# Interleaving the two MLP layers by half batch, with PSUM tiles drawn from one single-bank and one double-bank pool

## The chip, the cores and the metric

The kernel runs on one core of a Trainium2 chip. Its engines appear in the profile as PE (TensorE, matrix products and transposes), DVE (VectorE), ACT (ScalarE), POOL (GpSimd) and SP (SyncE, which here only issues DMAs). PE writes its results to PSUM; ACT and DVE read them from there and write to SBUF. The metric is the device time in microseconds (us), the median of three runs.

## The reference, cut to what matters

Inputs are `q`, `k` and `v` of shape 4 x 8 x 768 x 64 (batch, heads, positions, head width), all float32. Attention keeps, for each query, the 6 chunks of 32 keys with the highest upper bound; then a layer norm and a two-layer MLP follow, with a residual:

```python
k_min, k_max = min and max of k over each chunk of 32 keys
ub = sum(maximum(q * k_min, q * k_max), axis=-1)        # masked to causal chunks
top_chunks = argsort(ub)[..., -6:]
scores = (q @ k.T) / sqrt(64), kept where the key's chunk is selected and key <= query
attn_out = softmax(scores) @ v
x = attn_out as (4, 768, 512)
xn = (x - mean) / sqrt(var + 1e-6) * g_ln
out = x + maximum(xn @ w_ch1, 0) @ w_ch2                # 512 -> 2048 -> 512
```

## The kernel before

**Units of work.** Attention is cut into 16 groups `g`: batch `b = g // 4` and a pair of heads. A group's 768 positions are six tiles of 128, in two halves `r = 0, 1` of three tiles each. A group goes through `load_qk` and `load_v` (DMA), `prep_q` and `prep_k` (PE transposes into PSUM tiles `tr`, evacuated by ACT and DVE into the rings QA, QB, KA, KB), `bounds` (PE, tile `ub`), `select` (DVE), `mask_t` (PE transposes into `trh`, copied by DVE into QA and QB), and for each half `scores` (PE into tile `mm`, then an exponential on ACT into `pt`), `diag` (POOL zeroes the upper triangle of `pt`), `values` (PE into tile `sm`) and `normalise` (DVE divides and writes the group's columns of `x_all`).

**The MLP of a batch** follows when its four groups are done: `stats` (DVE: mean, variance and the centred `xc`), `x_t` (PE transposes of `xc` into `trh`, scaled into `xT` by DVE or ACT), `rstd` (DVE and POOL), `mlp1` (16 calls; each makes two 128-row slices of the hidden layer for one half, 8 matmuls into a tile `mm`, then a ReLU on ACT into `hT`), `mlp2` (24 calls; four calls of 4 matmuls make the 128 output rows of one position tile `s`, and after the fourth DVE adds the residual into `ot`, which SP stores to memory).

**PSUM.** There are three pools of two buffers. `ps_t` holds `tr` and both kinds of `trh`; `ps_s` holds `ub` and `sm`; `ps_m` holds tiles of `[P, 2, 512]` float32, a double bank each, shared by `scores`, `mlp1` and `mlp2`. A tile of `mlp2` (`yps[b]`, line 464) takes a whole double bank for two position tiles, so it stays open for eight calls:

```python
        if j == 0 and s % 2 == 0:
            yps[b] = ps_m.tile([P, 2, 512], F32, name="mm", tag="mm")
        yp = yps[b][:, s % 2]
```

**Order.** Every call is registered with a due time by `at(t, ...)`; the calls are issued in the order of these times, and a scheduler beneath them then settles the order of the instructions on each engine and hands a pool's free buffers to its tiles. An engine executes its instructions in that order. One unit of due time is one group. Group `g` starts its scores at `T = g - 4`, plus `GAP = 1.5` from the second batch on. The MLP of batch `b` is spread from the end of the attention of batch `b` to the end of that of `b + 1`: all 16 calls of `mlp1` in the first half of that time, all 24 of `mlp2` in the second. So the first batch's attention has no MLP beside it, the attention of batches 1 to 3 runs beside the MLP of the batch before, and the MLP of the last batch stands alone at the end (the tail). `x_all`, `xc`, `xT` and `hT` are tiles of a whole batch; `x_all` is float16.

Of the kernel before, what the change touches and what calls it, by code (L numbers as in the profile page):

```python
# [10 lines left out]
ALU = mybir.AluOpType  # L11
# [8 lines left out]
def kernel(  # L20
# [39 lines left out]
    ring = ctx.enter_context(tc.tile_pool(name="ring", bufs=1))  # L60
    ldp = ctx.enter_context(tc.tile_pool(name="ldp", bufs=4))
    vap = ctx.enter_context(tc.tile_pool(name="vap", bufs=5))
    prp = ctx.enter_context(tc.tile_pool(name="prp", bufs=2))
    smp = ctx.enter_context(tc.tile_pool(name="smp", bufs=2))
    ptp = ctx.enter_context(tc.tile_pool(name="ptp", bufs=2))
    xp = ctx.enter_context(tc.tile_pool(name="xp", bufs=2))
    xcp = ctx.enter_context(tc.tile_pool(name="xcp", bufs=1))
    htp = ctx.enter_context(tc.tile_pool(name="htp", bufs=1))
    outp = ctx.enter_context(tc.tile_pool(name="outp", bufs=2))

    PSUM = bass.MemoryType.PSUM
    ps_t = ctx.enter_context(tc.tile_pool(name="ps_t", bufs=2, space=PSUM))
    ps_s = ctx.enter_context(tc.tile_pool(name="ps_s", bufs=2, space=PSUM))
    ps_m = ctx.enter_context(tc.tile_pool(name="ps_m", bufs=2, space=PSUM))
# [13 lines left out]
    hsel = const.tile([P, 2], F32, name="hsel", tag="hsel")  # L88
    mhalf = const.tile([P, NT], F32, name="mhalf", tag="mhalf")
    NK = 5  # L90
    QA = [ring.tile([P, S], F16, name=f"QA{i}", tag=f"QA{i}") for i in range(NK)]
# [74 lines left out]

    def xb(b):
        if b not in x_tiles:
            x_tiles[b] = (
                xp.tile([P, NT, H, D], F16, name="x_all", tag="x_all"),  # L170
                xp.tile([P, KT1, S], F16, name="xT", tag="xT"),
            )
        return x_tiles[b]

# [23 lines left out]
    def turn(g, nm, t0, t1):  # L198
        pst = ps_t.tile([P, 512], F32, name="tr", tag="tr")
        src = st[g][nm]  # L200
        for t in range(t0, t1):
            nc.tensor.transpose(pst[:, (t - t0) * P:(t - t0 + 1) * P], src[:, t, :, :], ident_f)  # L202
        return pst[:, 0:(t1 - t0) * P]
# [65 lines left out]
    def bounds(g):  # L269
        p, bd = st[g], BD[g % NB]  # L270
        if g < HP:
            ub = ps_s.tile([P, NT - 1, 2, NCH], F32, name="ub", tag="sm")
            nc.tensor.matmul(
                ub.rearrange("p s h c -> p (s h c)"), ident_b, causb.rearrange("p s h c -> p (s h c)"),
                start=True, stop=False,
            )
            for s in range(1, NT):
                o = ub[:, s - 1].rearrange("p h c -> p (h c)")
                for nm, arr in (("q32", 0), ("r32", 1)):
                    nc.tensor.matmul(  # L280
                        o, p[nm][:, s * P:(s + 1) * P], bd[:, arr].rearrange("p h c -> p (h c)"),
                        start=False, stop=(s == NT - 1 and arr == 1),
                    )
        else:
            bh = BH[g % NB]
            ub = ps_s.tile([P, NT - 1, 2, 2, NCH], F32, name="ub2", tag="sm")
            for s in range(1, NT):
                o = ub[:, s - 1].rearrange("p l h c -> p (l h c)")
                for i, (nm, arr) in enumerate((("qh", 0), ("ql", 0), ("rh", 1), ("rl", 1))):
                    nc.tensor.matmul(  # L290
                        o, p[nm][:, s * P:(s + 1) * P], bh[:, arr].rearrange("p l h c -> p (l h c)"),
                        start=(i == 0), stop=(i == 3),
                    )
# [19 lines left out]
    def mask_t(g, i):  # L313
        mn = MN[i % NM]
        pm = ps_t.tile([P, S], F16, name="trh", tag="tr")
        for s in range(NT - 1):
# [60 lines left out]
    def values(g, r):  # L377
        pt, va = st[g]["pt", r], st[g]["va"]
        pv = ps_s.tile([P, 2, TR, D + 1], F32, name="sm", tag="sm")
        st[g]["pv", r] = pv  # L380
# [9 lines left out]
    def normalise(g, r):  # L390
        b, hp = divmod(g, HP)
        x_all, _ = xb(b)
        pv = st[g]["pv", r]
        rden = smp.tile([P, 2, TR, 1], F32, name="rden", tag="rden")
        nc.vector.reciprocal(rden, pv[:, :, :, D:D + 1])  # L395
        nc.vector.tensor_tensor(  # L396
            x_all[:, TR * r:TR * r + TR, 2 * hp:2 * hp + 2, :].rearrange("p s h d -> p h s d"),
            pv[:, :, :, 0:D], rden.to_broadcast([P, 2, TR, D]), ALU.mult,
# [3 lines left out]

    rs = {}

    def stats(b, t0, t1):
        x_all, _ = xb(b)
        if t0 == 0:
            rs[b] = dict(
                st=smp.tile([P, NT, nc.vector.BN_STATS_DIM], F32, name="bst", tag="bst"),
                mv=smp.tile([P, NT, 2], F32, name="mv", tag="mv"),  # L410
                rstd=smp.tile([P, NT], F32, name="rstd", tag="rstd"),
                xc=xcp.tile([P, NT, DM], F16, name="xc", tag="xc"),
            )
        r = rs[b]
        for s in range(t0, t1):
            xs = x_all[:, s].rearrange("p h d -> p (h d)")
            nc.vector.bn_stats(r["st"][:, s], xs)
            nc.vector.bn_aggr(r["mv"][:, s, :], r["st"][:, s])
            nc.vector.tensor_scalar(r["xc"][:, s, :], xs, r["mv"][:, s, 0:1], None, op0=ALU.subtract)

    def rstd(b, t0, t1):

        r = rs[b]
        c = slice(t0, t1)
        ve = smp.tile([P, NT], F32, name="ve", tag="ve")
        nc.vector.tensor_scalar(
            ve[:, c], r["mv"][:, c, 1], HS * HS, HS * HS * LN_EPS, op0=ALU.mult, op1=ALU.add,
        )
        nc.gpsimd.tensor_tensor(r["rstd"][:, c], ve[:, c], mhalf[:, c], ALU.pow)

    def x_t(b, kt, r):
        _, xT = xb(b)
        px = ps_t.tile([P, TR * P], F16, name="trh", tag="tr")
        for i in range(TR):
            nc.tensor.transpose(  # L435
                px[:, i * P:(i + 1) * P], rs[b]["xc"][:, TR * r + i, kt * P:(kt + 1) * P], ident_h,
            )
        c = slice(TR * r * P, TR * (r + 1) * P)
        if b == 0 and kt % 2 == 0:
            nc.scalar.activation(xT[:, kt, c], px, ACTF.Copy, scale=gstr[:, kt:kt + 1])  # L440
        else:
            nc.vector.tensor_scalar(xT[:, kt, c], px, gstr[:, kt:kt + 1], None, op0=ALU.mult)

    hts = {}

    def mlp1(b, r, m):
        _, xT = xb(b)
        if b not in hts:
            hts[b] = htp.tile([P, KT2, S], F16, name="hT", tag="hT")
        c = slice(TR * r * P, TR * (r + 1) * P)  # L450
        hp_ = ps_m.tile([P, 2, 512], F32, name="mm", tag="mm")
        for i in range(2):
            for kt in range(KT1):
                nc.tensor.matmul(  # L454
                    hp_[:, i, 0:TR * P], w1b[:, kt, (m + i) * P:(m + i + 1) * P],
                    xT[:, kt, c], start=(kt == 0), stop=(kt == KT1 - 1),
                )
        nc.scalar.activation(hts[b][:, m:m + 2, c], hp_[:, :, 0:TR * P], ACTF.Relu, scale=HS)  # L458

    yps = {}  # L460

    def mlp2(b, s, j):
        if j == 0 and s % 2 == 0:
            yps[b] = ps_m.tile([P, 2, 512], F32, name="mm", tag="mm")
        yp = yps[b][:, s % 2]
        for kt in range(4 * j, 4 * j + 4):
            nc.tensor.matmul(  # L467
                yp, hts[b][:, kt, s * P:(s + 1) * P], w2b[:, kt, :],
                start=(kt == 0), stop=(kt == KT2 - 1),
            )  # L470
        if j == 3:
            x_all, _ = xb(b)
            ot = outp.tile([P, DM], F32, name="ot", tag="ot")
            nc.vector.scalar_tensor_tensor(  # L474
                ot, yp, rs[b]["rstd"][:, s:s + 1], x_all[:, s].rearrange("p h d -> p (h d)"),
                op0=ALU.mult, op1=ALU.add,
            )
            nc.sync.dma_start(out[b, s * P:(s + 1) * P, :], ot)


    at(-9.0, consts_first)
    at(-8.95, g_load)
    GAP = 1.5
    for g in range(NG):
# [24 lines left out]
    for i in range(2, NK):  # L509
        at(-4.3 + 0.3 * i, ring_init, i)  # L510
    for b in range(B):
        e = 4.0 * b + (GAP if b > 0 else 0.0)
        for r in range(NR):
            f = e + (-0.56 if r == 0 else 0.0)
            for s in range(TR * r, TR * (r + 1)):
                at(f, stats, b, s, s + 1)
            for kt in range(KT1):
                at(f + 0.01, x_t, b, kt, r)
        at(e + 0.2, rstd, b, 0, NT)
        e = e + 0.05  # L520
        d = 4.0 * (b + 1) + GAP + 0.05 - e
        if b == B - 1:
            d = 4.0
        for m in range(KT2):
            at(e + 0.05 + 0.5 * d * m / KT2, mlp1, b, m // 8, 2 * m % KT2)
        for n in range(24):
            at(e + 0.06 + 0.5 * d + 0.5 * d * n / 24, mlp2, b, n // 4, n % 4)

# [32 lines left out]
```

## Time and profile before

| | us |
|---|---|
| runs | 330.22, 330.78, 332.76; median 330.78 |
| the profiled execution | 332.52 |
| its span, first to last instruction | 330.8 |
| PE, DVE, ACT, POOL busy in the span | 301.0, 203.9, 180.1, 74.0 |

The profiled execution is 1.7 us above the median and has 1.7 us around its span. Matrix products are pipelined: a product's own duration in the profile (326 ns for the first layer's) is longer than the time to the next one's start, so busy PE time says little, and the pace has to be read from starts. The largest groups by line, with the mean duration of one:

| line | what | count | mean ns |
|---|---|---|---|
| L454 | PE, first layer, 128x384 | 512 | 326 |
| L467 | PE, second layer, 128x512 | 384 | 379 |
| L359 | PE, scores | 448 | 251 |
| L385 | PE, values | 672 | 195 |
| L365 | ACT, exponential of scores | 96 | 916 |
| L458 | ACT, ReLU of the first layer | 64 | 810 |
| L474 | DVE, residual | 24 | 745 |
| L417, L418, L419 | DVE, stats | 24 each | 676, 164, 344 |
| L396 | DVE, normalise | 32 | 555 |

The DMAs move 26.65 MB, most of it in the first 75 us.

### The profile page before, as it was taken

The page shows a single profiled execution, that of the slowest core. Times are in us where ns is not written, and L with a number is a line of the kernel's source. Part 1 is how long each engine was busy: PE and PEld are TensorE (multiplying, and loading weights), DVE is VectorE, ACT ScalarE, POOL GpSimd, SP SyncE. Part 2 cuts the span into 40 slices and gives each one's busy share as a digit, 9 for nine tenths or more (in the row PEclk, how much of TensorE's full clock was granted, in tenths as well). Part 3 has the DMA queues.
Part 4 walks back from the last instruction along what each step waited for, and adds up shares of the span by engine and source line. Part 5 has one row for each costly group of instructions (what it writes and reads, how often), then busy time and mean ns, then how long its engine had stood idle before and what let it go on. Part 6 is the DMA issues. An engine that isn't in the chain of part 4 may idle for free.

```text
span 330.8 us, 6794 instructions
## 1 busy us (share of the span) xinstructions
PE 301.0 (91%) x2708; PEld 199.2 (60%) x2708; DVE 203.9 (62%) x657; ACT 180.1 (54%) x261; POOL 74.0 (22%) x116
## 2 busy tenths in 40 slices
PE   3879887999999998999999999999999999899994
PEld 2668675666675664666766565666656455565441
DVE  7766755998857779896564759886634336700121
ACT  2436759677975475358685625377775332366000
POOL 9714835211131422230313131120101020100000
PEclk9999989999999999999999999999999999999999
DMA  9997999963435636424523050000000101000021
GB/s 163 190 187 139 194 195 214 190 146 68 95 26 127 96 93 104 92 45 95 74 51 24 34 87 34 34 33 2 2 0 2 63 34 63 35 0 2 32 95 63
DMA packets 81967, 26.65 MB, mean 81 GB/s; under 512 B 76304, under 2 KB 78352, under 8 KB 81936
## 3 DMA queue, kind: packets, MB, share of 16 engines
q1 hardware_dynamic: 53632, 18.88, 24.1%
q0 software_dynamic: 27776, 7.34, 22.2%
q8 instruction: 21, 0.34, 0.5%
q10 hardware_dynamic: 528, 0.00, 0.1%
q14 instruction: 10, 0.08, 0.1%
HBM read 27.27 MB, written 6.29 MB: 101 GB/s over the span
## 4 chain that ended last, share of the span: by engine, by line
PE 60%; ACT 19%; DVE 15%; issue 2%; DMA 1%; SPq 0%; POOL 0%; ACTq 0%
PE mm L454 20%; PE mm L467 18%; ACT pt L365 8%; PE mm L359 6%; ACT hT L458 5%; PE sm L385 4%; PE ub L280 4%; PE tr L202 3%; ACT KB L254 3%; ACT KA L253 2%; DVE ot L474 2%; PE ub L290 2%; DVE kc L251 2%; DVE kc L252 2%; PE trh L435 2%
## 5 line engine op out<-in xcount | busy, mean ns | idle before, releaser
L365 ACT ACTIVATE pt<-mm 128x1024 f16<-128x1024 f32 x96 | 86.8, 916 | 52.1 <-PE mm L359 51.5
L454 PE MATMUL mm<-xT,w1b 128*128 128x384 f16 x512 | 93.3, 326 | 4.7 <-ACT hT L458 3.2
L467 PE MATMUL mm<-w2b,hT 128*128 128x512 f16 x384 | 92.7, 379 | 2.5 <-DVE ot L474 1.7
L458 ACT ACTIVATE hT<-mm 128x768 f16<-128x768 f32 x64 | 51.8, 810 | 40.7 <-PE mm L454 40.2
L454 PEld LDWEIGHTS <-w1b 128*128 128x128 f16 x512 | 49.0, 98 | 32.3 <-issue 5.5
L467 PEld LDWEIGHTS <-hT 128*128 128x128 f16 x384 | 36.6, 98 | 37.0 <-issue 3.7
L372 POOL TENSOR_SCALAR_AFFINE_SELECT pt<-pt 128x768 f16<-128x768 f16 x32 | 28.2, 880 | 115.4 <-ACT pt L365 115.4
L474 DVE SCALAR_TENSOR_TENSOR ot<-mm,rstd,x_all 128x512 f32<-128x512 f32 x24 | 17.9, 745 | 44.6 <-PE mm L467 43.1
L359 PE MATMUL mm<-QA,KA 128*128 128x128 f16 (+2 forms) x224 | 35.9, 251 | 5.2 <-ACT pt L365 4.3
L359 PE MATMUL mm<-QB,KB 128*128 128x128 f16 (+2 forms) x224 | 35.4, 252 | 0.0
L385 PE MATMUL sm<-va,pt 128*128 128x65 f16 x672 | 33.0, 195 | 2.3 <-ACT pt L365 1.8
L385 PEld LDWEIGHTS <-pt 128*128 128x128 f16 x672 | 28.4, 99 | 9.4 <-ACT pt L365 3.5
L193 POOL DMA_DIRECT2D va<-in_v_dram x32 | 28.2, 883 | 1.1 <-issue 0.2
L395 DVE RECIPROCAL rden<-sm 128x6 f32<-128x6 f32 x32 | 6.2, 193 | 33.5 <-PE sm L385 33.4
L253 ACT CAST KA<-tr 64x512 f16<-64x512 f32 (+1 forms) x32 | 15.0, 468 | 17.3 <-DVE kc L252 17.2
L359 PEld LDWEIGHTS <-KA 128*128 128x128 f16 x224 | 19.0, 102 | 8.9 <-issue 2.3
L202 PE MATMUL tr<-ident_f,qn 128*128 128x128 f32 x96 | 18.7, 303 | 5.9 <-DMA qn<-in_q_dram 5.1
L359 PEld LDWEIGHTS <-KB 128*128 128x128 f16 x224 | 18.6, 101 | 6.7 <-issue 4.2
L202 PE MATMUL tr<-ident_f,kn 128*128 128x128 f32 x96 | 19.7, 306 | 1.6 <-DMA kn<-in_k_dram 0.7
L251 DVE TENSOR_REDUCE kc<-tr 128x16 f32<-128x512 f32 (+1 forms) x32 | 17.7, 552 | 3.1 <-PE tr L202 2.9
L396 DVE TENSOR_TENSOR x_all<-sm,rden 128x384 f16<-128x384 f32 x32 | 17.7, 555 | 0.8
L226 DVE SCALAR_TENSOR_TENSOR q<-tr,q 128x384 f16<-128x384 f32 (+1 forms) x24 | 11.7, 488 | 9.9 <-ACT q L225 9.6
(79 smaller groups left out, 339.8 us busy)
## 6 DMA issues: line engine op xcount, KB each, us to landing
qn<-in_q_dram SPq DMA_DIRECT2D x32, 192.0 KB, 3.7
kn<-in_k_dram SPq DMA_DIRECT2D x32, 192.0 KB, 3.8
out_dram<-ot SPq DMA_DIRECT2D x24, 256.0 KB, 2.0
va<-in_v_dram POOLq DMA_DIRECT2D x32, 96.0 KB, 5.2
w1b<-in_moe_w_ch_dram POOLq DMA_DIRECT2D x4, 512.0 KB, 7.8
w2b<-in_moe_w_ch_dram POOLq DMA_DIRECT2D x4, 512.0 KB, 8.2
gstr<-in_moe_g_ln_dram ACTq DMA_DIRECT2D x1, 2.0 KB, 3.4
```

Of the source, the lines that this page charges most:

```text
L193: nc.gpsimd.dma_start(va[:, hh, t0:t1, 0:D], v[b, 2 * hp + hh, t0 * P:t1 * P, :].rearrange("(t p) d -> p t d", p=P),)
L202: nc.tensor.transpose(pst[:, (t - t0) * P:(t - t0 + 1) * P], src[:, t, :, :], ident_f)
L251: nc.vector.tensor_reduce(kc[:, 0, n], view, axis=AX.X, op=ALU.min)
L253: nc.scalar.copy(KA[g % NK][0:64, c], pst[0:64, :])
L359: nc.tensor.matmul(sc[:, hh, o:o + w * P], ks[:, t * P:(t + 1) * P], qs[:, s * P:(s + w) * P], start=True, stop=True,)
L365: nc.scalar.activation(pt[:, n0:n1].rearrange("p n h x -> p h n x"), sc[:, :, 0:o].rearrange("p h (n x) -> p h n x", x=P), ACTF.Exp, scale ...
L372: nc.gpsimd.affine_select(out=dv, in_=dv, compare_op=ALU.is_ge, fill=0.0, base=0, pattern=[[0, 2 * TR], [1, P]], channel_multiplier=-1,)
L385: nc.tensor.matmul(pv[:, hh, s2, :], pt[:, where[t, s], hh, :], va[:, hh, t, 0:D + 1], start=(t == 0), stop=(t == s),)
L454: nc.tensor.matmul(hp_[:, i, 0:TR * P], w1b[:, kt, (m + i) * P:(m + i + 1) * P], xT[:, kt, c], start=(kt == 0), stop=(kt == KT1 - 1),)
L458: nc.scalar.activation(hts[b][:, m:m + 2, c], hp_[:, :, 0:TR * P], ACTF.Relu, scale=HS)
L467: nc.tensor.matmul(yp, hts[b][:, kt, s * P:(s + 1) * P], w2b[:, kt, :], start=(kt == 0), stop=(kt == KT2 - 1),)
L474: nc.vector.scalar_tensor_tensor(ot, yp, rs[b]["rstd"][:, s:s + 1], x_all[:, s].rearrange("p h d -> p (h d)"), op0=ALU.mult, op1=ALU.add,)
```

## The change

The names in the diff are those of the program; `...` stands for what is left out, which renames tags (`"tr"` and `"sm"` become `"one"`) or indexes by half where it was by batch.

```diff
-    ldp = ctx.enter_context(tc.tile_pool(name="ldp", bufs=4))
+    ldp = ctx.enter_context(tc.tile_pool(name="ldp", bufs=3))
...
-    xp = ctx.enter_context(tc.tile_pool(name="xp", bufs=2))
-    xcp = ctx.enter_context(tc.tile_pool(name="xcp", bufs=1))
-    htp = ctx.enter_context(tc.tile_pool(name="htp", bufs=1))
+    xp = ctx.enter_context(tc.tile_pool(name="xp", bufs=5))
+    xcp = ctx.enter_context(tc.tile_pool(name="xcp", bufs=2))
+    htp = ctx.enter_context(tc.tile_pool(name="htp", bufs=2))
...
-    ps_t = ctx.enter_context(tc.tile_pool(name="ps_t", bufs=2, space=PSUM))
-    ps_s = ctx.enter_context(tc.tile_pool(name="ps_s", bufs=2, space=PSUM))
+    ps_t = ctx.enter_context(tc.tile_pool(name="ps_t", bufs=4, space=PSUM))
     ps_m = ctx.enter_context(tc.tile_pool(name="ps_m", bufs=2, space=PSUM))
...
-    NK = 5
+    NK = 4
...
-                xp.tile([P, NT, H, D], F16, name="x_all", tag="x_all"),
-                xp.tile([P, KT1, S], F16, name="xT", tag="xT"),
+            x_tiles[b, r] = xp.tile([P, TR, H, D], F32, name="x", tag="x")
...
-    def mlp2(b, s, j):
-        if j == 0 and s % 2 == 0:
-            yps[b] = ps_m.tile([P, 2, 512], F32, name="mm", tag="mm")
-        yp = yps[b][:, s % 2]
+    def mlp2(b, r, i, j):
+        h = hf[b, r]
+        if j == 0:
+            h["yp"] = ps_t.tile([P, DM], F32, name="yp", tag="one")
+        yp = h["yp"]
...
-    GAP = 1.5
+    GAP = 1.0
...
+    def spread(fn, b, r, lo, hi):
+        each = [(m,) for m in range(0, KT2, 2)] if fn == mlp1 else [(i, j) for i in range(TR) for j in range(4)]
+        for n, x in enumerate(each):
+            at(lo + (hi - lo) * n / len(each), fn, b, r, *x)
...
-        at(e + 0.2, rstd, b, 0, NT)
-        e = e + 0.05
-        d = 4.0 * (b + 1) + GAP + 0.05 - e
-        if b == B - 1:
-            d = 4.0
-        for m in range(KT2):
-            at(e + 0.05 + 0.5 * d * m / KT2, mlp1, b, m // 8, 2 * m % KT2)
-        for n in range(24):
-            at(e + 0.06 + 0.5 * d + 0.5 * d * n / 24, mlp2, b, n // 4, n % 4)
+            at(f + 0.2, rstd, b, r)
+        e += 0.06
+        z = 4.0 * (b + 1) + GAP + 0.06
+        m = e + GAP if b == 0 else (e + z) / 2
+        spread(mlp1, b, 0, e, m)
+        spread(mlp1, b, 1, m, z)
+        spread(mlp2, b, 0, m + 0.01, z)
+        spread(mlp2, b, 1, z + 0.01, z + 2.0)
```

In words: the MLP is handled by half batch. `mlp1` of half 0 runs in the first half of a batch's MLP time beside `mlp2` of half 1 of the batch before, and `mlp1` of half 1 runs in the second half of it beside `mlp2` of half 0. `mlp2` of half 1 moves past the start of the next batch, for the batch before the last into the tail. An output tile of `mlp2` is a single bank of its own, drawn from `ps_t`, which now serves every single-bank user (`tr`, `ub`, both `trh`, `sm`, `yp`) with four buffers; only `scores` and `mlp1` draw from the two double banks of `ps_m`. `x` is float32 and kept by half in five buffers; `xc`, `xT` and `hT` are by half in two buffers. The rings for q and k have four places in place of five, the loads of q and k three buffers in place of four, and `rstd` runs eight times on 3 columns in place of four times on 6. The number of matrix products is the same.

## The prediction

> **What bounds the kernel now.** I read the slices of the page first, then windows cut at the stages, then the order of PE's instructions by time.
>
> ```profile
> PE   3879887999999998999999999999999999899994
> ...
> PEclk9999989999999999999999999999999999999999
> ```
>
> PE is full from the seventh slice (50 us) to the last, at a granted clock of nearly 1 but for one slice. Cut where the first scores of a group or the last product of a stage stand, the span falls into start, gap, three attention batches with an MLP beside them, and tail:
>
> ```profile
> 0.00:59.00 59.00, 43.70 (x411) 35.85 (x412) 39.40 (x139) 32.86 (x49) 32.65 (x64) 0.97 1.30 183
> 59.00:81.40 22.40, 21.70 (x212) 15.35 (x210) 19.67 (x64) 16.03 (x28) 4.04 (x5) 1.00 0.78 140
> 81.40:141.90 60.50, 57.74 (x591) 38.11 (x589) 48.02 (x156) 36.76 (x54) 14.74 (x20) 1.00 0.51 91
> 141.90:214.80 72.90, 70.40 (x677) 46.52 (x675) 51.31 (x167) 43.92 (x64) 13.88 (x18) 1.00 0.28 50
> 214.80:282.30 67.50, 64.90 (x593) 40.99 (x592) 35.94 (x115) 37.59 (x51) 7.39 (x8) 1.00 0.07 24
> 282.30:330.80 48.50, 42.53 (x237) 22.34 (x234) 9.59 (x21) 12.96 (x16) 1.32 (x1) 0.99 0.10 39
> ```
>
> (The columns are length, then busy time of PE, weight loads, DVE, ACT, POOL, each with its count, then clock, share of the DMA engines, GB/s.) No other engine comes near PE in the fourth and fifth stage. But busy time hides how far PE is from its pace, so I take the pace from the tail, where nothing disturbs it:
>
> ```profile
> 287.19 17.71 PE L454 MATMUL mm<-xT,w1b 128*128 128x384 f16 x108
> 304.74 17.43 PE L467 MATMUL mm<-w2b,hT 128*128 128x512 f16 x80
> 323.01 3.61 PE L467 MATMUL mm<-w2b,hT 128*128 128x512 f16 x16 [0.84 <-DVE ot L474]
> ```
>
> 108 products of the first layer start in 304.74 - 287.19 = 17.55 us, 162.5 ns each; the second layer's take 216 ns by the same reading (12 in 2.59 us at 261.74). Undisturbed runs in the middle of the span give 30 ns for a values product (28 in 0.85 us), 42.5 for a bound (20 in 0.85 us), about 110 for a float32 transpose. One batch in the steady state then needs 128 x 0.1625 + 96 x 0.216 + 168 x 0.030 + 80 x 0.0425 + 48 x 0.11 = 55.2 us, plus scores by columns (4 groups x 5,376 columns x 0.1625/384 = 9.1) and 44 small transposes (2.4): 66.7 us. The chain of waits repeats itself with a period of 72.94 us (the same 16 first-layer products at 154.25 and 227.19). So PE loses 6.2 us, 8.5%, per batch; over the 200.9 us of the three middle stages 17 us. Where it loses them is seen in starts:
>
> ```profile
> 160.48 1.46 PE L454 MATMUL mm<-xT,w1b 128*128 128x384 f16 x8
> 161.78 0.27 PE L359 MATMUL mm<-QA,KA 128*128 128x256 f16 x1
> ...
> 162.21 0.23 PE L385 MATMUL sm<-va,pt 128*128 128x65 f16 x2
> 162.84 1.46 PE L454 MATMUL mm<-xT,w1b 128*128 128x384 f16 x8 [0.40 <-ACT hT L458]
> ...
> 167.85 1.46 PE L454 MATMUL mm<-xT,w1b 128*128 128x384 f16 x8
> ```
> ```profile
> 161.98 0.81 ACT L458 ACTIVATE hT<-mm 128x768 f16<-128x768 f32 x1 [1.22 <-PE mm L454]
> ...
> 166.99 0.81 ACT L458 ACTIVATE hT<-mm 128x768 f16<-128x768 f32 x1 [0.63 <-PE mm L454]
> ```
>
> The first ReLU ends at 162.79 and PE goes on at 162.84; the second at 167.80, PE at 167.85. The two double banks go round among first layer and scores, and a tile that comes 1.2 us after the one before it in its bank finds ACT still reading it. In the 17 us from 157 on, six such starts lose 1.8 us. In the second-layer half of a batch, 252 to 275, the output tile sits on one double bank for eight calls and scores have the other alone: 1.6 us lost there.
>
> **The change part by part.** All sums are against the profiled execution, 332.5 us, which is 1.7 above the median; differences are carried over to the median unscaled.
>
> *Double banks.* I laid the PE order of both built programs end to end at the paces above and took, for each tile from `ps_m` in the three middle stages, the PE work between the last product of the bank's tile before and its own first. ACT needs about 1.3 us (0.81 to 1.02, plus the product's own end). Before, 40 of 120 tiles have less, 19.5 us short in all; in the trace those 40 starts come 10.5 us late, as other work slips too. After, 15 of 112 have less, 8.2 us short. At the same ratio 4.4 us stay: **-6.1 us**. Bounds: 0 (what is late next is a DVE or ACT result, below) and -10.5.
>
> *Output tiles in single banks.* Within the second layer PE now waits for `ot` and hT in places that add up to 1.9 us in the middle stages (0.46 us at 261.74 is one). A new tile need not wait for the residual of the one before: **-1.0**, between 0 and -1.9.
>
> *Tail.* It has the two waits 0.96 us (first layer on ReLU, at 284.58) and 0.84 us (at 323.01, above); with four single banks and mixed layers both go: **-1.6**. 48 second-layer products of the third batch (10.4 us) move into it, but they leave the second stage of attention, so their own time cancels. The last tile's 16 products, residual and store still stand alone at the end.
>
> *Fewer products beside the second batch's attention.* PE has 44 second-layer products less there (9.5 us), 8 first-layer ones more (1.3), so about 52 us remain of 60.5, while DVE keeps some 46 of its 48.02 (three residuals at 0.745 fewer). DVE's busiest 20 us now are 18.26; 46 in 52 is 88%. More of PE's waits for DVE will show: **+1.5**, 0 to +4.
>
> *Float32 `x`.* Normalise, bn_stats and residual I leave at their size: bn_stats on float16 (676 ns for 512) is no faster per element than the two that read float32 from PSUM (745 for 512, 555 for 384). The centring at L419 has a float16 source now, 344 ns; L238 against L233 (640 elements, 321 ns float16, 482 float32) gives +0.25 ns per element, +0.13 us each, 24 times: 3.1 us on DVE, of which only the three before a half's transposes can hold PE, and the MLP covers them: **+0.5**, 0 to +3.1.
>
> *Start and loads.* In PE's order the first transposes of group 4 move ahead of group 3's last scores. Their load is issued at 48.5 and 49.0 us, behind POOL's copy of a group-3 result, and lands 3.2 to 7.2 us later; PE gets there at about 54, so PE, and ACT behind it, can stand 0 to 3 us: +1.0. Against it, transposes wait 5.4 us in the first 60 us for ACT to empty the two buffers of `ps_t` (KB 2.4 + 0.9, q 1.6 + 0.5); four shared ones save some: -1.0, -3 to 0. Together **0**. SP's stores of `ot` move between other loads, but with three buffers a load may go up to three groups (some 50 us) ahead of its transposes, which hides that; fewer buffers for q and k and the fourth ring place act in the same slack. `rstd` puts four more POOL instructions (1.39 us for 6 columns) in front of `diag`, on whose end values have waited 1.0 us in all: **+0.2**, 0 to +2.
>
> The sum is -6.1 - 1.0 - 1.6 + 1.5 + 0.5 + 0 + 0.2 = -6.5 us: 330.8 - 6.5 = **324.3 us**.
>
> One rule speaks against the gain: in the Trainium skill, "TensorE: Matmul & The Clock Gate", in the section on how HAM oscillation bites, adding PSUM double-buffering to a kernel whose PE is kept warm gave no further gain. Here the clock is warm throughout the middle stages too, and the rule alone would make the first term 0 and the sum -0.4. I follow the trace, in which PE's start sits 0.05 us behind ACT's end.
>
> Another is from "PSUM — Partial Sum Buffer", summary of rules: evacuate promptly. An output tile is now open in a single bank while about 9 us of other PE work pass (by the order); no row prices that, and the second rival below is what it could lead to.
>
> **The rivals.** *The wait only changes its name.* Once a bank is free, the product waits for what ACT and DVE still owe: ACT is 60% and DVE 70% busy in the fourth stage, both in order. For it: in the start, where no MLP fills, PE waits mostly for data. Against it: the six starts above each end with the bank's own reader. Then the first two terms vanish, leaving -6.5 + 7.1 = +0.6: 331.4.
>
> *Slower: `ps_t` runs dry at the half boundaries.* The new order opens three or four transposes of `xc` at once, one per `kt`, in all single banks that are free, tile by tile as DVE centres them; until the third is centred no other transpose, bound, values or output tile can start, and PE's queue stands behind. A half's chain on DVE is 0.75 (normalise) + 3 x (0.68 + 0.17 + 0.47) = 4.7 us. It happens seven times before the tail. For it: PE's weight loads already wait 5.1 us, 12 times, for L419. Against it: the order puts 2 to 4 us of products in front. It outweighs the gain from 0.9 us each on, and 2 us each gives 324.3 + 14 = 338.
>
> *All of it is won.* If nothing of the 17 us and the tail's 1.8 stays: 312.
>
> That the layers are not mixed is excluded: the built order alternates 8 first-layer with 4 second-layer products.
>
> **How the numbers follow.** Forecast 0.58, all won 0.08, wait renamed 0.20, dry pool 0.14. One per cent, 3.3 us, is what a measurement can tell from no change. The first two are faster: 0.66, same 0.20, slower 0.14. All favourable bounds together give -10.5 - 1.9 - 1.6 - 2 = -16.0, 315; the unfavourable ones, with the first two terms as forecast, -8.7 + 4 + 3.1 + 3 + 2 = +3.4, 334. 315 to 333 holds the forecast, the renamed wait and the shallow end of the dry pool; outside are its deep end and the case in which all is won.
>
> **What will show it.** In the changed profile the period of a batch between equal products should fall from 72.9 to about 70.5; first-layer starts right behind a ReLU's end should be few; "ACT hT" and "ACT pt" should lose share in the chain; the tail should have no idle of PE above 0.3 us before its last tile. Waits of the `xc` transposes or of `tr` above 1 us at half boundaries would show the dry pool; an unchanged period with PE behind DVE, the renamed wait. A start stage longer than 62 us would make the term for loads wrong.

## The result and the profile after

| | us |
|---|---|
| before | median 330.63 (330.22 to 332.76) |
| after | median 334.93 (334.72 to 335.40, 4 runs) |
| ratio | 1.0119, 95% interval 1.0074 to 1.0163 |
| the profiled execution after, and its span | 334.97, 333.2 |

The changed kernel is 1.2% slower where 2% faster was forecast, and its time lies outside the range. The slices of its page say where:

```profile
PE   3768873699999999779999999899999999999994
...
PEclk9999998759999999999999999999999999999999
```

PE is 0.3 busy in the seventh slice (50 to 58 us), and the clock falls to 0.5 in the ninth (67 to 75 us). From there on PE is full, but for two slices at 0.7 at the border of the third batch's attention (133 to 150 us). The windows of the changed kernel, cut at the first scores of groups 3 and 4 and at the end of the attention (columns as in the prediction):

```profile
0.00:50.40 50.40, 35.17 (x333) 29.59 (x333) 35.08 (x122) 26.77 (x43) 27.69 (x59) 1.00 1.18 166
50.40:86.50 36.10, 27.11 (x236) 19.20 (x237) 24.46 (x75) 19.13 (x30) 7.41 (x11) 0.81 0.89 132
...
276.00:333.20 57.20, 53.01 (x286) 26.91 (x282) 12.32 (x25) 12.98 (x16) 0.85 (x1) 1.00 0.12 46
```

The same two cuts of the kernel before:

```profile
0.00:52.30 52.30, 38.91 (x335) 32.30 (x336) 35.31 (x127) 27.00 (x43) 29.26 (x59) 0.97 1.27 180
52.30:77.90 25.60, 23.45 (x244) 16.24 (x245) 21.51 (x67) 19.44 (x31) 6.57 (x9) 1.00 1.09 176
```

Group 4's first scores come at 86.5 us, before at 77.9: 8.6 us later, although group 3's come 1.9 us earlier. The rest of the span is 246.7 us where it was 252.9: 6.2 us shorter. The two make the 2.4 us between the spans. So the change earns about what it was forecast to earn, and loses more in the 36 us between group 3 and group 4. The medians lie further apart, 4.3 us, because the profiled execution before is 1.9 us above its median; it has 3.4 us at a granted clock of 0.50 (from 46.57 us on), and executions of that kernel with a mean clock of 0.999 take 330.2 to 330.8 us.

To compare kernels whose orders differ, I take each PE instruction in its order, add up the work before it at the prediction's undisturbed paces, and call the difference to its real start the time lost. The whole program is 272.1 us of such work in both kernels, and some 4.3 us of last residual and store follow it.

| us lost by PE | before | after | difference |
|---|---|---|---|
| up to group 3's first scores | 26.8 | 24.9 | -1.8 |
| from there to group 4's | 4.6 | 16.3 | +11.7 |
| groups 4 to 7 | 6.3 | 4.6 | -1.7 |
| groups 8 to 11 | 7.2 | 7.2 | 0.0 |
| group 12 to the first scores of 15 | 5.7 | 2.7 | -3.0 |
| group 15 and tail | 3.9 | 1.0 | -2.9 |

The timeline of PE in the changed kernel shows the second row:

```profile
52.25 0.27 PE L355 MATMUL mm<-QB,KB 128*128 128x256 f16 x1
57.24 1.08 PE L198 MATMUL tr<-ident_f,qn 128*128 128x128 f32 x4 [4.72 <-DMA qn<-in_q_dram]
...
59.40 1.06 PE L198 MATMUL tr<-ident_f,kn 128*128 128x128 f32 x4
60.26 0.63 PE L198 MATMUL tr<-ident_f,qn 128*128 128x128 f32 x2
...
66.00 0.40 PE L428 MATMUL trh<-ident_h,xc 128*128 128x128 f16 x4 [2.42 <-DVE xc L413]
...
70.27 5.09 PE L443 MATMUL mm<-xT,w1b 128*128 128x384 f16 x21
```

In order of time: PE stands 4.72 us at group 4's first transposes, with group 3's remaining scores behind them in its queue. Then four transposes take 0.86 us from start to start, 215 ns each in place of 110, and 21 first-layer products take 4.92 us (the next instruction starts at 75.19), 234 ns in place of 162.5: about half pace. In between PE waits 2.42 us for `xc`. DVE has the tiles of the next batch's first group in hand (kc, q and r of group 4) ahead of the statistics of the first batch. Of the 15.9 us lost between 52.1 and 86.5, the load takes 4.9, the waits for DVE and ACT around 66 us 3.4, the slow pace between 57.2 and 75.2 the other 6.3, and later small waits 1.3.

The granted clock (the third column from the right) in windows of the same stretch, cut where it changes:

```profile
52.87:56.28 3.41, 0.00 (x0) 0.00 (x0) 0.09 (x1) 1.06 (x2) 2.08 (x3) 1.00 1.33 183
56.28:59.69 3.41, 2.45 (x16) 2.35 (x17) 0.56 (x1) 0.99 (x2) 0.00 (x0) 0.50 1.66 158
59.69:63.11 3.42, 3.16 (x25) 2.41 (x24) 2.54 (x7) 2.12 (x4) 0.86 (x1) 0.50 1.52 207
63.11:66.52 3.41, 0.86 (x6) 0.30 (x5) 3.41 (x10) 2.69 (x4) 0.00 (x0) 1.00 1.08 211
66.52:69.93 3.41, 2.85 (x34) 2.48 (x35) 2.84 (x10) 1.29 (x3) 0.89 (x1) 0.50 0.43 87
69.93:73.35 3.42, 3.42 (x20) 1.84 (x18) 3.03 (x10) 0.79 (x3) 1.86 (x3) 0.50 0.99 147
```

In the Trainium skill, "TensorE: Matmul & The Clock Gate", what's actually happening, the clock goes to half after an idle window of about 3.4 us and back after as long a busy one; the wait of 4.72 us and the half pace behind it agree with that. The page's re-warm time alone would cost about 1.7 us (an estimate: half of 3.4); the trace has 6.3. The clock stands at 0.50 for 6.8 us behind the wait, is back for one window in which PE is busy only 0.86 us (the waits around 66 us), and stands at 0.50 for another 6.8 us.

The load that PE waited for stands in the chain of waits of the changed kernel, behind POOL's issue of the second layer's weights:

```profile
44.34 0.76 POOL w2b L160
...
48.08 9.03 DMA qn<-in_q_dram
```

It was issued at 48.08 (before: 48.5) and landed 9.0 us later (before: 5.0). Before, the last of the weights were issued at 40.97, now at 44.34, and took 10.3 us to land at the median. That the load is late because it shares the DMA engines with them is likely, not shown: it landed after 8.0 to 9.1 us in experiments 1, 2 and 4 below, whose last weights were issued at 43.3 to 44.4, and after 6.9 and 7.7 in 3 and 5, where that was at 40.1 and 40.0. (By the slices of the page before, half of the 26.65 MB moves in the first 74 us, not most of it.)

In the middle the new order parts the users of the double banks as the prediction had it. The place in the third batch's attention, PE and then ACT of the changed kernel:

```profile
160.24 1.46 PE L443 MATMUL mm<-xT,w1b 128*128 128x384 f16 x8
161.54 1.03 PE L455 MATMUL yp<-w2b,hT 128*128 128x512 f16 x4
...
164.37 1.46 PE L443 MATMUL mm<-xT,w1b 128*128 128x384 f16 x8
```
```profile
161.74 0.81 ACT L447 ACTIVATE hT<-mm 128x768 f16<-128x768 f32 x1 [0.64 <-PE mm L443]
```

The ReLU ends at 162.55, the next first-layer tile starts at 164.37: four second-layer products and scores lie between, and no first-layer start sits right behind a ReLU's end here. Waits of the first layer for ReLU fall from 3.2 us in the page before to 0.7; scores still wait for a ReLU five times between 86 and 276 us, 1.9 us in all. The tail ends without a gap before its last tile:

```profile
317.62 11.39 PE L455 MATMUL yp<-w2b,hT 128*128 128x512 f16 x52
```

### The profile page after: what moved, and what is told of

It is laid out like the page before. It is cut to its first block, busy times and chain, and to the rows that moved or that the text cites. A ratio compares the mean times of both kernels' runs of the same rounds, so it can differ in the third digit from the quotient of the medians.

```text
span 333.2 us, 6796 instructions
## 1 busy us (share of the span) xinstructions
PE 297.6 (89%) x2708; PEld 198.4 (60%) x2708; DVE 210.7 (63%) x657; ACT 181.9 (55%) x261; POOL 73.6 (22%) x120
## 4 chain that ended last, share of the span: by engine, by line
PE 58%; DVE 20%; ACT 11%; DMA 4%; issue 4%; POOL 2%; SPq 0%; ACTq 0%; POOLq 0%; DVEq 0%
PE yp L455 19%; PE mm L443 18%; PE mm L355 6%; ACT pt L361 4%; PE tr L198 4%; PE sm L381 4%; DVE bst L411 3%; PE ub L286 3%; DMA qn<-in_q_dram 3%; PE ub L276 3%; ACT KB L250 2%; DVE kc L248 2%; DVE kc L247 2%; ACT hT L447 2%; ACT KA L249 2%
## 5 line engine op out<-in xcount | busy, mean ns | idle before, releaser
L361 ACT ACTIVATE pt<-mm 128x1024 f16<-128x1024 f32 x96 | 85.7, 917 | 35.5 <-PE mm L355 33.6
L443 PE MATMUL mm<-xT,w1b 128*128 128x384 f16 x512 | 98.1, 330 | 1.3 <-ACT hT L447 0.7
L455 PE MATMUL yp<-w2b,hT 128*128 128x512 f16 x384 | 96.5, 379 | 0.0
L461 DVE SCALAR_TENSOR_TENSOR ot<-yp,rstd,x 128x512 f32<-128x512 f32 x24 | 18.0, 748 | 51.0 <-PE yp L455 49.3
L355 PE MATMUL mm<-QB,KB 128*128 128x128 f16 (+2 forms) x224 | 36.1, 251 | 0.0
L381 PEld LDWEIGHTS <-pt 128*128 128x128 f16 x672 | 26.4, 100 | 7.3 <-ACT pt L361 1.6
L381 PE MATMUL sm<-va,pt 128*128 128x65 f16 x672 | 28.8, 197 | 1.3 <-ACT pt L361 0.3
L189 POOL DMA_DIRECT2D va<-in_v_dram x32 | 27.0, 850 | 0.7
L222 DVE SCALAR_TENSOR_TENSOR q<-tr,q 128x384 f16<-128x384 f32 (+1 forms) x24 | 11.7, 489 | 15.9 <-ACT q L221 15.9
L198 PE MATMUL tr<-ident_f,kn 128*128 128x128 f32 x96 | 18.6, 307 | 2.4 <-DMA kn<-in_k_dram 2.0
L221 ACT ACTIVATE q<-tr 128x512 f16<-128x512 f32 (+1 forms) x24 | 11.8, 491 | 15.0 <-PE tr L198 14.8
## 6 DMA issues: line engine op xcount, KB each, us to landing
w2b<-in_moe_w_ch_dram POOLq DMA_DIRECT2D x4, 512.0 KB, 10.3
```

The source lines that it names most:

```text
L189: nc.gpsimd.dma_start(va[:, hh, t0:t1, 0:D], v[b, 2 * hp + hh, t0 * P:t1 * P, :].rearrange("(t p) d -> p t d", p=P),)
L355: nc.tensor.matmul(sc[:, hh, o:o + w * P], ks[:, t * P:(t + 1) * P], qs[:, s * P:(s + w) * P], start=True, stop=True,)
L361: nc.scalar.activation(pt[:, n0:n1].rearrange("p n h x -> p h n x"), sc[:, :, 0:o].rearrange("p h (n x) -> p h n x", x=P), ACTF.Exp, scale ...
L381: nc.tensor.matmul(pv[:, hh, s2, :], pt[:, where[t, s], hh, :], va[:, hh, t, 0:D + 1], start=(t == 0), stop=(t == s),)
L443: nc.tensor.matmul(hp_[:, i, 0:TR * P], w1b[:, kt, (m + i) * P:(m + i + 1) * P], h["xT"][:, kt], start=(kt == 0), stop=(kt == KT1 - 1),)
L455: nc.tensor.matmul(yp, h["hT"][:, kt, i * P:(i + 1) * P], w2b[:, kt, :], start=(kt == 0), stop=(kt == KT2 - 1),)
```

## The experiments

Each ratio is to the kernel before on the same chip, with its 95% interval; "lost early" is PE's time lost up to group 4's first scores, "lost later" from there to the end, both from the one profiled execution (before: 31.3 and 23.1; after: 41.3 and 15.5).

| | median us | ratio | lost early | lost later |
|---|---|---|---|---|
| 1 after, group 4 prepared later | 328.52 | 0.9891 (0.9820 to 0.9961) | 35.9 | 16.3 |
| 2 after, GAP 1.5 | 329.77 | 0.9944 (0.9899 to 0.9989) | 31.9 | 17.8 |
| 3 before, GAP 1.0 | 341.46 | 1.0313 (1.0220 to 1.0407) | 35.7 | 25.9 |
| 4 before, new pools | 333.85 | 1.0063 (1.0022 to 1.0103) | 33.6 | 20.6 |
| 5 after, GAP 1.5, old pools | 339.31 | 1.0223 (1.0173 to 1.0272) | 29.3 | 32.1 |
| 6 after, GAP 1.5, x float16 | 328.32 | 0.9885 (0.9836 to 0.9933) | 33.5 | 17.2 |
| 7 after, GAP 1.5, xc transposes later | 329.63 | 0.9913 (0.9869 to 0.9957) | 36.3 | 16.7 |
| 8 after, group 4 loaded earlier | 328.43 | 0.9912 (0.9876 to 0.9947) | 34.7 | 15.6 |
| 9 edits of 6, 7, 8, GAP 1.0 | 325.59 | 0.9808 (0.9759 to 0.9856) | 32.8 | 14.4 |
| 10 edits of 6, 7, 8, GAP 1.5 | 327.33 | 0.9841 (0.9791 to 0.9892) | 34.1 | 15.2 |
| 11 edits of 6, 7, GAP 1.5 | 327.08 | 0.9842 (0.9784 to 0.9901) | 33.8 | 15.2 |
| 12 after, GAP 1.5, outputs in double banks | 347.49 | 1.0470 (1.0403 to 1.0537) | 32.9 | 36.8 |

"Lost early" varies by some microseconds with where the clock falls, in kernels whose start hardly differs (2, 6, 7, 11: 31.9 to 36.3); only larger steps in it are read. The profiled execution is also not always a usual one: it lies 1.8 and 1.4 us above the median in experiments 1 and 7, and 2.0, 1.8 and 1.5 us below it in 2, 3 and 4.

### The start

**1.** Group 4's preparation alone is due half a group later:

```diff
+        w = T + (0.5 if g == HP else 0.0)
-            at(T - (1.6 if first else 1.98) + 0.09 * t0, prep_q, g, t0, t1)
+            at(w - (1.6 if first else 1.98) + 0.09 * t0, prep_q, g, t0, t1)
...
-        at(T - (0.45 if first else 0.45), mask_t, g, g)
+        at(w - (0.45 if first else 0.75 if g == HP else 0.45), mask_t, g, g)
```

(prep_k, prep_q2, prep_b, bounds and select take `w` in the same way; mask_t moves by 0.2.)

> The changed kernel with the due times of one group's preparation (group 4: its transposes, bounds, selection) 0.5 later, nothing else. Theory A: the start is lost because GAP 1.0 put group 4's transposes ahead of group 3's last scores in PE's order, so that PE stood 4.7 us on their load and then ran at half clock. Then no PE wait for that load above 1 us is left, the granted clock stays at 1.0 from 55 to 75 us, group 4's first scores start near 78 us (86.5 in the changed kernel, 77.9 before), and the time is 325 to 328 us. Theory B: the load itself is late (second-layer weights issued 3.4 us later, 9.0 us to land), whatever PE's order is. Then PE waits at another place and the time stays at 332 to 335 us.

328.52 us, 6.4 below the changed kernel and half a microsecond above the range of the theory that put the loss there. 5.4 of it are in "lost early". PE waits for no load at the transposes any more, though the load still took 8.0 us; but the clock fell all the same, at another place (0.50 in the window from 50 to 56 us), and group 4's first scores came at 81.0, not near 78.

**2.** `GAP = 1.0` becomes `GAP = 1.5`, as before the change.

> The changed kernel with GAP 1.5 in place of 1.0, the whole schedule after the first batch shifted with it. Theory A: as in e1, 325 to 328 us, since the constant is what moved the transposes. Theory B: 332 to 335 us. If e1 is fast and this is not, the constant is not the cause but the place of group 4 alone.

329.77 us. Group 4's scores come at 77.2, before at 77.9, and the early loss is that of the kernel before, 31.9 against 31.3. The load still took 9.1 us to land, but PE reached it later and waited for nothing there. So most of the excess goes with the GAP: the pools, the mixed layers and the smaller rings are all still there, and the time falls by 5.2 us. Not all of it does. This execution is 2.0 us below the median of its kernel, that of the kernel before 1.9 above; by the medians the kernel is only 1.1 us faster than the one before, though it loses 5.3 us less later, so some 4 us more are lost early in a usual execution (an estimate from these numbers). The later loss is 17.8, 2.3 more than with 1.0, so the shorter GAP also earned something.

**3.** The kernel before with the GAP of the change, `GAP = 1.0`, and nothing else.

> The kernel before with GAP 1.0 in place of 1.5, nothing else. Theory A: this one constant brings the loss of the start into the kernel before: PE waits several us for group 4's load, the clock falls after it, 335 to 341 us. Theory B: 329 to 332 us, as the loads and the PSUM pools are those of before.

341.46 us, 3% slower and just above the range: the GAP alone harms the old kernel more (10.6 us) than the new one (5.2). By the trace 4.4 us of it are lost early and 2.8 later, so this is not the loss of the start alone. Its PE timeline has the same wait, shorter:

```profile
54.04 1.09 PE L202 MATMUL tr<-ident_f,qn 128*128 128x128 f32 x4 [2.39 <-DMA qn<-in_q_dram]
```

**8.** In the changed kernel the load of group 4 is let go one group earlier, everything else as it is:

```diff
-                nc.gpsimd.tensor_copy(st[g][nm][0:1, 0, 0, 0:1], st[HP - 1]["m8"][0:1, 0, 0, 0:1])
+                nc.gpsimd.tensor_copy(st[g][nm][0:1, 0, 0, 0:1], st[HP - 2]["m8"][0:1, 0, 0, 0:1])
```

> The changed kernel, GAP 1.0 as it is, with the loads of q and k of group 4 let go by the second-last instead of the last group of the first batch, so that they land before the first transposes of group 4 stand at the head of PE's queue. Theory L (the time lost in the start is the wait of 4.7 us for that load and the lower clock after it): 326 to 330 us, no wait of PE over 2 us at these transposes and no granted clock under 0.8 after them. Rival W (the earlier loads take their time from the weights of the layers, and the same time is lost to those, or to VectorE doing group 4's tiles ahead of xc): 332 to 336 us.

328.43 us, 6.5 below the changed kernel, and 6.6 of "lost early". PE's timeline:

```profile
50.29 0.41 PE L198 MATMUL tr<-ident_f,qn 128*128 128x128 f32 x2
...
57.63 0.32 PE L355 MATMUL mm<-QA,KA 128*128 128x384 f16 x1 [1.24 <-ACT pt L361]
...
60.11 0.61 PE L428 MATMUL trh<-ident_h,xc 128*128 128x128 f16 x4 [2.00 <-DVE xc L413]
```

The transposes stand even further forward, at 50.29 where PE had stood from 52.5 to 57.24, and wait for nothing. This is the load's wait taken away with the GAP kept, and it returns two thirds of the 9.9 us. What stays is the wait for `xc`, 2.00 us, as DVE still has group 4's tiles ahead of it (1.44 us in experiment 2, where it has not), and a clock of 0.88 from 50.6 to 80.0. The expectation of no clock under 0.8 was wrong: it was 0.74 from 56 to 62 us and 0.69 from 62 to 68. The rival's collision exists (the second layer's weights take 13.7 us to land, 10.3 in the changed kernel) and costs nothing that shows.

### The pools and the mixed layers

**4.** The kernel before, its order of layers kept, with the new pools and the output tile in a single bank:

```diff
-    ps_t = ctx.enter_context(tc.tile_pool(name="ps_t", bufs=2, space=PSUM))
-    ps_s = ctx.enter_context(tc.tile_pool(name="ps_s", bufs=2, space=PSUM))
+    ps_t = ctx.enter_context(tc.tile_pool(name="ps_t", bufs=4, space=PSUM))
...
-        if j == 0 and s % 2 == 0:
-            yps[b] = ps_m.tile([P, 2, 512], F32, name="mm", tag="mm")
-        yp = yps[b][:, s % 2]
+        if j == 0:
+            yps[b] = ps_t.tile([P, DM], F32, name="yp", tag="one")
+        yp = yps[b]
```

> The kernel before with the PSUM pools of the change alone: one pool of four single banks for all single-bank tiles, an output tile of the second layer in a single bank of it, two double banks for scores and the first layer; the order by batch, float16 x and GAP 1.5 stay. Theory M: the middle's gain is the double banks that the output tiles no longer hold; the second-layer halves lose their waits, the first-layer halves keep theirs, 326 to 328.5 us. Rival N: it takes the mixing of the layers to part the users of the double banks; pools alone give 329 to 332 us.

333.85 us, above both ranges: no gain, rather 0.6% lost. The trace, of the fastest of ten executions, has 2.5 us less lost later and 2.3 more early. This kernel's last weights were issued at 44.4 us, as in every kernel with one pool of four single banks (43.2 to 44.7); with the old pools it was at 40.0 to 41.0 (before, 3, 5). So the late weights come with the pools and not with the mixed order or the GAP, and part of what is lost early may come with them; no run takes the two apart.

**5.** The other half: the mixed order with the pools of before (GAP 1.5, to be held against 2).

```diff
-    ps_t = ctx.enter_context(tc.tile_pool(name="ps_t", bufs=4, space=PSUM))
+    ps_t = ctx.enter_context(tc.tile_pool(name="ps_t", bufs=2, space=PSUM))
+    ps_s = ctx.enter_context(tc.tile_pool(name="ps_s", bufs=2, space=PSUM))
...
-        if j == 0:
-            h["yp"] = ps_t.tile([P, DM], F32, name="yp", tag="one")
-        yp = h["yp"]
+        if j == 0 and i % 2 == 0:
+            h["yp"] = ps_m.tile([P, 2, 512], F32, name="mm", tag="mm")
+        yp = h["yp"][:, i % 2]
```

(`ub`, `ub2` and `sm` draw from `ps_s` again.)

> The changed kernel with GAP 1.5 and with the PSUM pools of the kernel before: two banks for transposes, two for scores' small tiles, two double banks shared by the first layer and the second layer's outputs. The order of the layers stays mixed. Theory M (mixed order needs the pools: with shared double banks each first-layer pair must wait for an output pair that lies open over 32 products, so the wait for the eviction comes back): 333 to 340 us. Rival N (the mixed order alone makes the gain seen with GAP 1.5, 329.8 us, and the pools add nothing, as they added nothing to the kernel before): 328 to 331 us. In the profile M shows first-layer products waiting for ACT's hT, N does not.

339.31 us: the mixed order by itself is 2.2% slower than the kernel before, with 32.1 us lost later against 17.8 in 2.

**12.** Of 5 only the second hunk: output pairs in the double banks, the four single banks kept.

> The changed kernel with GAP 1.5 and one edit: the second layer's output tiles lie in the double banks again, in pairs, as in the kernel before; transposes, bounds and small score tiles keep the four single banks. Theory shared (with the mixed order an open output pair holds one of the two double banks for up to 32 products, and the first-layer pairs and scores between them have only the other; this is what made the kernel with all the old pools 339.3 us): 336 to 340 us, the products of scores and of the first layer waiting for ACT as there. Rival small pool (the two banks of transposes and the two of small tiles were what was short there): 329 to 331 us.

347.49 us, beyond even the upper end. This one edit costs 19 us after group 4. Its groups by line, against 0.7 and 7.8 us of idle time in the same two groups of experiment 2:

```profile
L443 PE MATMUL mm<-xT,w1b 128*128 128x384 f16 x512 | 95.2, 327 | 7.1 <-ACT pt L361 6.0
...
L355 PE MATMUL mm<-QA,KA 128*128 128x128 f16 (+2 forms) x224 | 35.9, 249 | 11.5 <-ACT pt L361 7.1
```

These two groups hold some 10 of the 19 us. How it comes about is seen in PE's timeline and then ACT's:

```profile
117.11 0.38 PE L355 MATMUL mm<-QA,KA 128*128 128x128 f16 x2 [0.64 <-ACT pt L361]
...
118.57 0.32 PE L355 MATMUL mm<-QA,KA 128*128 128x384 f16 x1 [0.83 <-ACT hT L447]
...
119.48 1.01 PE L455 MATMUL mm<-w2b,hT 128*128 128x512 f16 x2 [0.43 <-ACT pt L361]
```
```profile
117.71 0.81 ACT L447 ACTIVATE hT<-mm 128x768 f16<-128x768 f32 x1
```

The ReLU ends at 118.52 and the scores start at 118.57; the same release with the exponential at 117.05 and 117.11. An output pair stays open over eight calls spread through the half batch, so scores and first layer have one double bank between them for that time, and their tiles wait for ACT to empty the last. Why 12 is slower than 5, which has the same output pairs and fewer shared single banks, is not settled.

### The smaller terms

**6.** `x` in float16 as before the change (GAP 1.5): `xp.tile([P, TR, H, D], F32, ...` becomes `F16`.

> The changed kernel with GAP 1.5 and x kept in float16, as the kernel before keeps it. It measures the prediction's term for float32 x (0.5 us, bounds 0 to 3.1) against the same order with float32, 329.8 us. Theory small (VectorE's x operations lie beside PE's work): 328.5 to 330.5 us. Rival large (VectorE is on the path at the half boundaries, so that its shorter operations on x show in full): 326 to 328 us.

328.32 us, between the two ranges; its interval overlaps that of experiment 2, so the times alone don't tell the size. The trace gives 0.65 us less lost later, which is the small theory's order.

**7.** The transposes of the second halves' `xc` come later:

```diff
-                at(f + 0.01, x_t, b, r, kt)
+                at(f + (0.01 if r == 0 else 0.3), x_t, b, r, kt)
```

> The changed kernel with GAP 1.5 and with the transposes of the centred x of every second half due 0.29 later, so that the first one does not stand in PE's queue before VectorE has written xc. Theory boundary (the wait of 1.9 us of the first such transpose at the border of batch 0 and batch 1, and the smaller ones after it, are on PE's path): 326 to 328.5 us. Rival renamed (the products behind it find the same xc late, or the next wait ends last): 329 to 331 us.

329.63 us, no difference that shows: the rival's range. The trace has 1.1 us less lost later, and more lost early, where its clock fell to 0.50 (window from 50 to 56 us).

**9 to 11.** The three edits together, with both GAPs, and two of them without the earlier load.

> The changed kernel, GAP 1.0, with three edits together: group 4's loads let go one group earlier, x in float16, and the transposes of the second halves' centred x due 0.29 later. Theory additive (the earlier load is worth 6.5 us as measured alone, x in float16 0.65 us and the later transposes 1.1 us by the stretch from group 4 to the end of their traces): 325 to 328 us. Rival absorbed (the start varies by several us with the granted clock, and what the two small edits free is taken up there): 328 to 330 us.

> The same three edits with GAP 1.5. Theory additive (with GAP 1.5 the transposes of group 4 stand behind the second scores of group 3 already, so the earlier load adds nothing to the wait, but the two small edits count): 326 to 328.5 us. Rival early load harms (it takes bandwidth from the weights of the layers without a wait to remove): 329 to 331 us.

> The changed kernel with GAP 1.5, x in float16 and the later transposes, the loads of group 4 as they are. Theory additive (329.8 us less 0.65 and 1.1 us): 327 to 328.8 us. Rival absorbed by the start: 329 to 330.5 us. Beside the kernel with the earlier load it tells what that load is worth at GAP 1.5.

325.59, 327.33 and 327.08 us, all three in the additive range. The best one beats the kernel before by 1.9% (1.4 to 2.4), and the changed kernel by 3.1% by the two ratios; the median of the kernel before was 332.5 us beside these three and 330.6 to 330.9 beside the others, and against those the gain would be some 1.6%. With GAP 1.5 the earlier load is worth nothing: there is no wait for it to remove. That GAP 1.0 is better than 1.5 once the load is early is likely (14.4 against 15.2 lost later), but the intervals overlap.

## Why the prediction was wrong

**The step that failed** is *Start and loads*: "PE, and ACT behind it, can stand 0 to 3 us: +1.0", set off against shorter waits of transposes and put down as 0 in all. The mechanism was named, the size was wrong: by group 4's first scores the changed kernel has lost 9.9 us more (41.3 against 31.3), although the other half of the term came (-1.8 up to group 3's scores, where -1.0 was put down). Three things make up most of the difference.

- The stand itself was 4.7 us, over the bound. The bound took the landing times of before, 3.2 to 7.2 us; the load now took 9.0, most likely since the weights were issued 3.4 us later and were still moving. And PE got there at 52.5 us, not at 54. A duration under load was carried over as if it were a constant.
- The price of what stands behind was left out. After the stand the clock was at 0.50 for 13.7 us in two stretches up to 73.4, and the slow pace took 6.3 us in all; the profile of before showed one slice at a granted clock of 0.8, and the prediction passed over it.
- The GAP moves all of group 4's preparation, not only PE's part. DVE's work on it came ahead of `xc`, and PE waited there too; experiment 8 shows that with 2.00 us left when the load is early. It is the smallest of the three, as 1.44 us of this wait stand with GAP 1.5 too.

Experiments 1, 2 and 8 each take the early transposes or their load away in another manner and return 5.2 to 6.5 us; experiment 3 shows a wait for the load, of 2.39 us, and an early loss in a kernel that has nothing else of the change. The rest of the excess, 3 to 5 us in experiments 1 and 8 by their traces, stays open: the clock falls in the start of those kernels too, and what the late weights do there no run isolates. The range, besides, ended at 333, while its own unfavourable bounds came to 334 with the two largest savings still in.

**The other terms hold together.** After group 4 the sum forecast was -6.5, measured -7.6. Up to group 15's first scores it was -4.9 (-6.1, -1.0, +1.5, +0.5, +0.2), measured -4.7; the tail -1.6, measured -2.9 with group 15's attention in it. The period between equal scores (first of group 9 to first of 13) fell from 73.0 to 70.4 us, forecast 70.5. The tail has no idle time of PE. That the sums match so well is in part luck, as the parts below show.

**Their split does not hold.** Double banks and output tiles were priced as two savings that add, -6.1 and -1.0. Experiments 4, 5 and 12 show one saving with two conditions. Pools alone bring nothing in the time (2.5 us after group 4 by the trace), the mixed order alone costs 9 us later than group 4, and the edit that was put at -1.0 decides over 19 us as soon as the layers are mixed. The sum came right because both were reckoned on the built order of the whole change. Two passages of the Trainium skill that the prediction weighed can be placed now. That double-buffering PSUM gave no further gain in a kernel whose PE stayed warm ("TensorE: Matmul & The Clock Gate", how HAM oscillation bites): the time of experiment 4 is in line with it, while in the mixed order the pools are worth 9.5 us (experiments 2 and 5). Evacuating promptly ("PSUM — Partial Sum Buffer", summary of rules): the open output pairs in the double banks of experiment 12, which cost 19 us, agree; in the four single banks the second layer's products wait 0.0 us in the page after, and no run isolates what an open tile costs there.

**Float32 `x`**: centring takes 476 ns at the mean in the changed kernel and took 344, +0.13 us as worked out; the term of +0.5 compares with 0.65 from experiment 6, one trace each.

**Fewer products beside the second batch's attention**, +1.5: groups 4 to 7 lost 1.7 us less. What was feared came one batch later, from group 8's to group 9's first scores, 5.3 us lost where it was 2.9.

**The rivals.** The renamed wait is out: starts moved, and the period with them. Transposes of `xc` stand over 1 us at two of the seven borders: 2.42 us at 66.00 (above), and at the border of group 8, where PE's timeline of the changed kernel shows

```profile
145.04 0.40 PE L428 MATMUL trh<-ident_h,xc 128*128 128x128 f16 x4 [1.68 <-DVE xc L413]
```

The dry pool at 2 us for each border is not what happened; its 338 lies nearest to the time measured by luck, for another reason. The slower side had its true mechanism in the list of terms, bounded at 3 us, where it should have been a rival: a stand of PE with a price for what follows it. The sign of it that was written down, a start stage over 62 us, is there plainly: the first first-layer product comes at 70.3, before at 60.5.

## What to carry to other kernels

Where an edit moves an instruction forward in an in-order queue, find when its data lands in the new order, with the other loads issued by then, and price all that stands behind it, the lower clock after the stand included. Two edits that remove the same wait are not two terms: price each with the other undone, or put them down as one. A tile that stays open across interleaved work takes its buffer away from everybody else for all that time, so spread-out accumulation wants its own small pool.

## What the runs showed of the hardware

The granted clock fell in the start of almost every kernel, also where PE stood for no long time. The windows that show it are the 3.41 us ahead of a fall. In the changed kernel PE did nothing in one of them (52.87 to 56.28, above). In the kernel before it was busy 2.17 us (43.16 to 46.57), with no wait over 1.24 us, and in experiment 1 2.38 us (42.85 to 46.26). The idle window of some 3.4 us that "TensorE: Matmul & The Clock Gate" names in the section cited above was not there in these two as one wait; the measurement decides, and what set these two off is open. Experiment 5 shows no fall from 24 us to the end of the start, with PE no busier (5.93 of 8 us from 42 to 50), and has the smallest early loss of all, 29.3 us. Ahead of that the clock's row can't be trusted: it says 1.00, but 20 bounds of experiment 5 start some 215 ns apart from 13.42 us on, and some 113 ns apart from 24.79 on.
